# A fused attention and expert kernel: logits with the tokens in the rows, and the first expert's tokens selected in two parts

## The chip, the cores and the metric

The kernel runs on one core of one Trainium2 chip. The metric is the time in microseconds (us) that the device needs for one execution; less is better. The engines are TensorE (PE in the profile; its weight loads are listed apart as PEld), VectorE (DVE), ScalarE (ACT), GpSimd (POOL), and SyncE (SP), which issues most transfers. Each engine works off its own instructions in order and waits for the others on semaphores, so an instruction that has to wait holds everything that stands behind it on its engine.

## The reference, cut to what matters

Three stages follow each other: attention with a sliding window (2 x 8 heads, 768 positions, 64 wide), a dense layer pair on the resulting 1536 x 512 tokens, and a layer in which each token goes to one of eight experts, or to none.

```python
x = attention(q, k, v)               # 1536 tokens x 512
x = np.maximum(0.01 * (x @ w_in), x @ w_in) @ w_out        # 512 -> 2048 -> 512
do_compute = (x @ w_skip) > 0
logits = x[do_compute] @ w_gate      # 8 experts
e_idx = np.argmax(logits, axis=1)
gate_w = softmax(logits)[e_idx]
for e in range(8):                   # w1[e]: 512 x 1024, w2[e]: 1024 x 512
    h = np.maximum(xc[e_idx == e] @ w1[e], 0.0)
    y[e_idx == e] = gate_w * (h @ w2[e])
out = x;  out[do_compute] = x[do_compute] + y
```

All is float32. The kernel gets that precision from a faster product format (written fp32r in the rows) by cutting each operand into a high part and a low part, what the high part leaves over, and adding three products: high by high, low by high, high by low.

## The kernel before, in words

The 1536 tokens are six groups of 256, each two tiles of 128. While group g goes through the dense layers, the attention of group g+1 is done between its products. A group takes 16 chunks (`chunk`): 12 products of 256 columns into `h` (L835), four passes on ACT and DVE that make the high and low part of the activation, and six products of 512 columns into the two sums `acc`, one for each tile (L856). For the last four chunks of the last group the products into the second tile's sum are put off (`self.rest`), so that the first tile's sum is complete earlier.

When a group's sums are complete, `gating` works out where each token goes. The sums are copied to `x2`, one half by ACT (L902) and one by DVE (L904), and stored. PE transposes the tile (L918, four transposes), ACT and DVE make the high and low part `xh` of the transposed tile (L921, L922). Twelve products (L930) then take `w9`, the nine columns of `w_skip` and `w_gate`, as the weights and 128 tokens as the moving columns, so that the logits come out as 9 rows of 128 tokens; ACT copies them (L935), and PE transposes them back (L937), so that DVE finds the tokens in the rows. DVE takes the maximum (L947), the comparison with zero (L948), the first expert that has the maximum (L950, L952), and its one-hot row (L954). PE counts how many tokens of each expert stand ahead of each token (L977: products of bf16 ones and a triangle with the one-hot rows), DVE reads the token's rank out of the counts (L983), and POOL scatters the tokens to the experts' lists `scr` in DRAM (L994). The last group's two tiles go through `gating` one after the other.

An expert then reads its list `xs` back from DRAM. For the first expert that way round would be too long: its list as it stood before the last group is read ahead (`first_rows`), and the tokens of the last two tiles are added by products (`first_x`). `sel` holds for each tile a 128 x 128 matrix of zeros and ones, made by DVE from the ranks (L987), that puts the tile's tokens into the expert's slots. PE writes `xs` transposed into four sums, one for each quarter of the model width (L817: plain float32, four products, which run as two instructions each), and adds both tiles' tokens (L819: eight products, 16 instructions). ACT and DVE cut the four sums into high and low part `xt` (L1088, L1089), and the first expert's 24 products of 512 columns start (L1060).

The experts' weights come as 16 sets (two for each expert) of four chunks of 512 KB. SP loads each chunk into one of four buffers `wm`; ACT makes the high part (L701) and DVE, or POOL for the last chunk of a set, the low part (L708), into two of 32 buffers `w`. A chunk's `wm` buffer is free when its low part is made, and a `w` buffer when PE has used it. An expert's second layer is L1076.

The order on each engine isn't written out: every operation is entered with an engine, an assumed cost and a priority `pr` (`Plan.op`), a planner plays them through (`Plan.run`), starting on each engine the ready operation of least priority whose buffers are free, and the program is written in that order. So a change of one cost, dependence or buffer can move instructions on every engine from that place on.

## Time and profile before

| what | us |
|---|---|
| median of 3 runs | 563.36 (563.24 to 564.45) |
| the profiled execution | 565.15 |
| its span, from the first to the last instruction | 563.3 |
| PE busy | 523.5 (93%) |
| PE weight loads | 458.1 (81%) |
| DVE busy | 406.2 (72%) |
| ACT busy | 345.9 (61%) |
| POOL busy | 170.0 (30%) |
| chain that ended last: PE | 60% of the span |
| chain that ended last: DVE, ACT, DMA, POOL | 12%, 9%, 8%, 6% |

The profiled execution is one of its own and 1.79 us above the median of the three timed runs; durations are read from it, and differences are taken from the median. The span is almost the whole of its time. Busy times of PE overlap, since its products are pipelined: two products of 0.39 us that follow each other start 0.23 us apart. So the distance between starts is what counts.

### The profile page before, as it was taken

How to read it: one execution, taken by the hardware profiler on the slowest of the kernel's cores; microseconds unless marked ns; L12 is line 12 of the kernel's file. 1: busy time of each engine (PE TensorE's matmuls, PEld its weight loads, DVE VectorE, ACT ScalarE, POOL GpSimd, SP SyncE). 2: the span in 40 equal slices, each digit the busy share in tenths (PEclk: the TensorE clock that was granted, in tenths of full speed). 3: DMA queues.
4: the chain of work that ended last, by engine and by line, in shares of the span. 5: the costliest groups of instructions: out<-in, count | busy, mean ns of one | idle time of the engine just before them, and what ended most of it. 6: DMA issues, size and time to landing. Idle time of an engine off the chain costs nothing.

```text
span 563.3 us, 10312 instructions
## 1 busy us (share of the span) xinstructions
PE 523.5 (93%) x3370; PEld 458.1 (81%) x3370; DVE 406.2 (72%) x1160; ACT 345.9 (61%) x889; POOL 170.0 (30%) x285
## 2 busy tenths in 40 slices
PE   4899999999999999989999999999999889999993
PEld 2778998888888898978888888998887768888771
DVE  3899999997767677777577776756855566776761
ACT  3998766654665566675566765556456267666660
POOL 4322022130353143333233332220321214434343
PEclk9999999999999999999999999999999699999997
DMA  7998345330111112221112320117465277787870
GB/s 181 286 324 282 119 153 158 115 104 20 34 38 43 51 40 47 49 76 43 29 41 47 85 48 3 25 37 219 144 212 171 84 283 249 256 272 270 259 229 20
DMA packets 78912, 72.47 MB, mean 129 GB/s; under 512 B 56403, under 2 KB 64595, under 8 KB 78848
## 3 DMA queue, kind: packets, MB, share of 16 engines
q1 hardware_dynamic: 76560, 70.54, 40.8%
q0 software_dynamic: 1600, 1.04, 0.6%
q8 instruction: 29, 0.48, 0.3%
q14 instruction: 35, 0.29, 0.2%
q10 hardware_dynamic: 688, 0.13, 0.1%
HBM read 65.40 MB, written 10.51 MB: 135 GB/s over the span
## 4 chain that ended last, share of the span: by engine, by line
PE 60%; DVE 12%; ACT 9%; DMA 8%; POOL 6%; issue 4%; POOLq 0%; SPq 0%; ACTq 0%; DVEq 0%
PE h L835 17%; PE acc L856 14%; DMA wm<-in_moe_w_dram 5%; PE acc L1076 3%; PE PV L655 3%; PE T L616 3%; POOL w L708 3%; ACT P L588 2%; PE h L1060 2%; PE S L582 2%; PE S L1060 2%; PE T L930 2%; DVE C L671 1%; PE PV L1060 1%; DVE P L585 1%
## 5 line engine op out<-in xcount | busy, mean ns | idle before, releaser
L835 PE MATMUL h<-x,w 128*128 128x256 f32 x1128 | 155.2, 286 | 1.0 <-DVE gl L849 0.9
L835 PEld LDWEIGHTS h<-x,w 128*128 128x128 f32 x1128 | 144.0, 190 | 5.3 <-DVE gl L849 1.3
L856 PE MATMUL acc<-w,gh 128*128 128x512 f32 x308 | 100.1, 406 | 0.2 <-ACT gh L848 0.2
L701 ACT ACTIVATE w<-wm 128x1024 fp32r<-128x1024 f32 x64 | 67.9, 1061 | 43.9 <-DMA wm<-in_moe_w_dram 27.5
L708 DVE TENSOR_TENSOR w<-wm,w 128x1024 fp32r<-128x1024 f32 x48 | 61.9, 1302 | 20.6 <-ACT w L701 18.8
L588 ACT ACTIVATE P<-P,s 128x272 f32<-128x272 f32 (+1 forms) x96 | 50.1, 523 | 27.9 <-DVE s L585 26.8
L708 POOL TENSOR_TENSOR w<-wm,w 128x1024 fp32r<-128x1024 f32 x16 | 38.7, 2416 | 89.1 <-ACT w L701 47.6
L600 POOL TENSOR_SCALAR P<-P,s 128x272 f32<-128x272 f32 (+1 forms) x72 | 36.5, 518 | 93.8 <-DVE s L593 74.9
L856 PE MATMUL acc<-w,gl 128*128 128x512 f32 x156 | 61.4, 394 | 0.0
L856 PEld LDWEIGHTS acc<-w,gh 128*128 128x128 f32 x308 | 53.3, 189 | 8.0 <-ACT gh L848 0.6
L846 ACT ACTIVATE t<-h 128x256 f32<-128x256 f32 x94 | 35.6, 379 | 34.8 <-PE h L835 34.5
L847 DVE TENSOR_TENSOR h<-h,t 128x256 f32<-128x256 f32 x94 | 40.1, 427 | 20.8 <-ACT t L846 20.0
L848 ACT ACTIVATE gh<-h 128x256 fp32r<-128x256 f32 x92 | 34.8, 378 | 21.0 <-DVE h L847 20.4
L849 DVE TENSOR_TENSOR gl<-h,gh 128x256 fp32r<-128x256 f32 x92 | 38.5, 419 | 10.2 <-ACT gh L848 9.5
L585 DVE CUSTOM_DVE_ANT_0 P<-S,mk 128x272 f32<-128x272 f32 (+1 forms) x70 | 28.9, 413 | 11.4 <-PE S L582 7.9
L856 PEld LDWEIGHTS acc<-w,gl 128*128 128x128 f32 x156 | 29.3, 188 | 7.4 <-DVE gl L849 0.8
L616 PE MATMUL T<-idt,P 128*128 128x128 f32 x152 | 27.1, 295 | 7.1 <-DVE kT L503 3.2
L616 PEld LDWEIGHTS T<-idt,P 128*128 128x128 f32 x152 | 22.3, 205 | 13.0 <-POOL P L600 4.1
L672 POOL TENSOR_TENSOR xr<-C 128x128 f32<-128x128 f32 x32 | 15.6, 488 | 43.2 <-DVE C L671 43.0
L671 DVE TENSOR_TENSOR C<-PV,C 64x256 f32<-64x256 f32 x48 | 20.2, 422 | 11.2 <-ACT C L670 8.1
L622 ACT ACTIVATE AT<-T 128x256 fp32r<-128x256 f32 x60 | 20.0, 382 | 13.4 <-PE T L616 13.1
L623 DVE TENSOR_TENSOR AT<-T,AT 128x256 fp32r<-128x256 f32 x60 | 23.3, 419 | 6.0 <-ACT AT L622 5.7
(264 smaller groups left out, 1081.0 us busy)
## 6 DMA issues: line engine op xcount, KB each, us to landing
wm<-in_moe_w_dram SPq DMA_DIRECT2D x64, 512.0 KB, 4.7
w<-in_moe_w_in_dram SPq DMA_DIRECT2D x14, 512.0 KB, 6.3
w<-in_moe_w_out_dram SPq DMA_DIRECT2D x14, 512.0 KB, 7.3
rq<-in_q_dram SPq DMA_DIRECT2D x56, 64.0 KB, 2.2
out_dram<-x SPq DMA_DIRECT2D x12, 256.0 KB, 2.8
rk<-in_k_dram SPq DMA_DIRECT2D x24, 96.0 KB, 2.4
rv<-in_v_dram SPq DMA_DIRECT2D x24, 96.0 KB, 2.3
scr<-x SPq DMA_DIRECT2D x1, 2056.0 KB, 9.4
```

The costliest lines, as they stand in the source:

```text
L585: P.op("DVE", 66 + 1.07 * ncol, lambda sp=sp, h=h: nc.vector.tensor_tensor_reduce(out=A.tile[:, 0:ncol, h], in0=sp.tile[:, 0:ncol], in1=ma ...
L588: P.op("ACT", 280 + 0.83 * ncol, lambda h=h: nc.scalar.activation(out=A.tile[:, 0:ncol, h], in_=A.tile[:, 0:ncol, h], func=AF.Exp, scale=- ...
L600: P.op("POOL", 245 + 0.83 * ncol, lambda h=h: nc.gpsimd.tensor_scalar(out=A.tile[:, 0:ncol, h], in0=A.tile[:, 0:ncol, h], scalar1=sm.tile[ ...
L616: nc.tensor.transpose(tt.tile[:, 2 * j + h, :], A.tile[:, o:o + 128, h], c["idt"])
L701: nc.scalar.activation(out=at(0), in_=view(src.tile), func=AF.Copy)
L708: P.op(lo, {"DVE": c_dve(n), "POOL": c_pool2(n)}[lo], lambda: eng[lo].tensor_tensor(out=at(1), in0=view(src.tile), in1=at(0).bitcast(F32), ...
L835: nc.tensor.matmul(out=h.tile, lhsT=wi.tile[:, a, 128 * k:128 * k + 128], rhs=xT.tile[:, b, k, :], start=k == 0 and n == 0, stop=k == self ...
L846: P.op("ACT", c_act(256, True), lambda: nc.scalar.activation(out=t.tile, in_=h.tile, func=AF.Copy, scale=0.01), r=[h], w=[t], pr=fast)
L847: P.op("DVE", c_dve(256), lambda: nc.vector.tensor_tensor(out=h.tile, in0=h.tile, in1=t.tile, op=ALU.max), r=[t], w=[h], pr=fast)
L848: P.op("ACT", c_act(256, True), lambda: nc.scalar.activation(out=gh.tile, in_=h.tile, func=AF.Copy), r=[h], w=[gh], pr=fast)
L849: P.op("DVE", c_dve(256), lambda: nc.vector.tensor_tensor(out=gl.tile, in0=h.tile, in1=gh.tile.bitcast(F32), op=ALU.subtract), r=[h, gh], ...
L856: nc.tensor.matmul(out=acc[i].tile, lhsT=a.tile[:, q], rhs=wo.tile[:, b, :], start=first and n == 0, stop=last and n == 2)
```

## The change

The logits change sides: the tile `xh` becomes the weights and `w9`, widened by a column of zeros to ten, the moving columns. The result stands with the tokens in the rows at once, in one tile `lt`; the copy L935 and the transposes L937 go. Products that need only the high part of `xh` come first.

For the first expert, `xs` and the two tiles of tokens are cut into high and low part as rows, ahead of the selection (`split_rows`: ACT makes the high part, DVE the low part of `xs`, POOL that of the tiles), and the selection is done on both parts with fp32r products: 8 for each of the three sources, for two sums `hi` of two quarters each and one `lo`. What was the cut after the selection is now two copies by ACT and two by DVE. `sel` is made from the counts (`cp`) directly, ahead of the rank.

`idle` adds products of bf16 ones, 128 x 128, that nobody reads: 6 after the last product of the second tile's sum, 12 after its logits, 5 after its count, 5 after the selection. And the third and fourth chunk of the third expert's first set are cut only after the first expert's `xt` (`after=[first]`), the fourth one's low part by DVE, not POOL.

```diff
     def gating(self, g, acc, own):
...
-        lp = P.buf("T", [9, 128 * n])
+        lt = P.buf("T", [128, n, 10])
...
-            for h in range(parts):
-                ks = range(4 // parts * h, 4 // parts * (h + 1))
-
-                def lg(m=m, xh=xh, ks=ks):
-                    for k in ks:
-                        for j, (a, b) in enumerate(((0, 0), (1, 0), (0, 1))):
-                            nc.tensor.matmul(out=lp.tile[:, 128 * m:128 * m + 128], lhsT=self.w9[:, a, k, :], rhs=xh.tile[:, b, 128 * k:128 * k + 128],
-                                             start=k == 0 and j == 0, stop=k == 3 and j == 2)
-
-                P.op("PE", 3 * len(ks) * 54, lg, r=[(xh, (0, h)), (xh, (1, h)), "w9"], w=[lp], pr=pr)
-        ls = P.buf("wl", [9, 128 * n])
-        P.op("ACT", c_act(128 * n, True), lambda: nc.scalar.activation(out=ls.tile, in_=lp.tile, func=AF.Copy), r=[lp], w=[ls], pr=pr)
-        lt = P.buf("T", [128, n, 9])
-        P.op("PE", 30 * n, lambda: [nc.tensor.transpose(lt.tile[:, m, :], ls.tile[:, 128 * m:128 * m + 128], c["idt"][0:9, 0:9]) for m in range(n)], r=[ls], w=[lt], pr=pr)
+            for b, ws in ((0, (0, 1)), (1, (0,))):
+                for h in range(parts):
+                    ks = range(4 // parts * h, 4 // parts * (h + 1))
+
+                    def lg(m=m, xh=xh, ks=ks, b=b, ws=ws):
+                        for k in ks:
+                            for a in ws:
+                                nc.tensor.matmul(out=lt.tile[:, m, :], lhsT=xh.tile[:, b, 128 * k:128 * k + 128], rhs=self.w9[:, a, k, :],
+                                                 start=k == 0 and a == 0 and b == 0, stop=k == 3 and b == 1)
+
+                    made = P.op("PE", len(ws) * len(ks) * 57, lg, r=[(xh, (b, h)), "w9"], w=[lt], pr=pr)
+        if self.fast and last and own == [1]:
+            self.idle(12, made)
...
     def first_rows(self):
...
+        self.xa = P.buf("gT", [128, 2, 2, 4, 128], F32R)
+        self.split_rows(self.xs0, [self.xs0], self.xa, 0, lambda i: self.xa.tile[:, 0, i], pr)
+
+    def split_rows(self, x, rd, dst, n, at, pr, lo="DVE", after=()):
+
+        P, nc = self.p, self.nc
+        cols = lambda: x.tile[:, 0:512].rearrange("p (f k) -> p k f", k=4)
+        P.op("ACT", c_act(512, False), lambda: nc.scalar.activation(out=at(0), in_=cols(), func=AF.Copy), r=rd, w=[(dst, (n, 0))], pr=pr, after=after)
+        P.op(lo, c_dve(512) if lo == "DVE" else c_pool2(512), lambda: (nc.vector if lo == "DVE" else nc.gpsimd).tensor_tensor(out=at(1), in0=cols(), in1=at(0).bitcast(F32), op=ALU.subtract), r=rd + [(dst, (n, 0))], w=[(dst, (n, 1))], pr=pr)
+
+    def first_x(self, x2, high):
...
+        hi, lo = [P.buf("h", [128, 2, 128]) for _ in range(2)], P.buf("acc", [128, 2, 2, 128])
...
+                    P.op("PE", 2 * 60, lambda i=i, j=j: [nc.tensor.matmul(
+                        out=self.x0[i][j][2]()[:, k, :], lhsT=at(i)[:, 2 * j + k, :], rhs=sel.tile[:, col, :], start=n == 0 and k == 0 and not (i and j), stop=n == 2 and k == 1 and (j == 1 or not i)) for k in range(2)],
+                        r=[(x, (1 if n else 0, i))] + rd, w=[self.x0[i][j][0:2]], pr=pr)
...
+    def idle(self, n, done):
+
+        nc, x, ones = self.nc, self.spare, self.c["ones"]
+        self.p.op("PE", n * 57, lambda: [nc.tensor.matmul(out=x.tile[:, 0:128], lhsT=ones, rhs=ones, start=True, stop=True) for _ in range(n)], w=[x], pr=self.KF * self.NG, after=[done])
...
     def plan_routed(self):
...
-                self.split(raw, hl, lambda i, hl=hl: hl[i].tile, 1024, pr + 0.3 * n, "ACT", "DVE" if n != 3 else "POOL")
+                self.split(raw, hl, lambda i, hl=hl: hl[i].tile, 1024, pr + 0.3 * n, "ACT", "DVE" if n != 3 or (e, m) == (2, 0) else "POOL", after=[first] if (e, m) == (2, 0) and n > 1 else ())
...
-                for k, x in enumerate(self.x0):
-                    self.split_psum(x, (xt, k), lambda i, xt=xt, k=k: xt.tile[:, i, k], 128, N - 9)
+                for j in range(2):
+                    P.op("ACT", c_act(256, True), lambda xt=xt, j=j: nc.scalar.activation(out=xt.tile[:, 0, 2 * j:2 * j + 2, :], in_=self.x0[0][j][2](), func=AF.Copy), r=[self.x0[0][j][0:2]], w=[(xt, (2 * j, 0)), (xt, (2 * j + 1, 0))], pr=N - 9)
+                    first = P.op("DVE", c_dve(256), lambda xt=xt, j=j: nc.vector.tensor_copy(xt.tile[:, 1, 2 * j:2 * j + 2, :], self.x0[1][j][2]()), r=[self.x0[1][j][0:2]], w=[(xt, (2 * j, 1)), (xt, (2 * j + 1, 1))], pr=N - 9)
```

What the planner makes of it is shown at three places. On PE, around the last product of the second tile's sum: `acc_5663` is that sum before and `acc_5641` after, `T_6242` and `T_6214` hold the first tile's transposes, and L930 and L971 are the logits. Before:

```order
L856 MATMUL acc_5663<-w_1818,xr_6197 128x512 x2
L856 MATMUL acc_5663<-w_1818,gl_6209 128x512
L817 MATMUL acc_6238<-idt,xs_5967 128x128
L918 MATMUL T_6242<-idt,x_1270_5901 128x128 x4
L856 MATMUL acc_5663<-w_1892,gh_6204 128x512 x2
L856 MATMUL acc_5663<-w_1892,gl_6213 128x512
L930 MATMUL T_6258<-wl_6243,w_75 9x128 x6
L817 MATMUL acc_6266<-idt,xs_5967 128x128
L930 MATMUL T_6258<-wl_6243,w_75 9x128 x6
L918 MATMUL T_6277<-idt,x_1283_5965 128x128 x4
L937 MATMUL T_6284<-idt,wl_6275 128x9
L930 MATMUL T_6296<-wl_6278,w_75 9x128 x12
```

After (L893 is L856, L957 is L918, L840 the selection, L857 the products that nobody reads):

```order
L893 MATMUL acc_5641<-w_1809,xr_6179 128x512 x2
L893 MATMUL acc_5641<-w_1809,gl_6191 128x512
L957 MATMUL T_6214<-idt,x_1260_5880 128x128 x2
L893 MATMUL acc_5641<-w_1895,gh_6186 128x512 x2
L893 MATMUL acc_5641<-w_1895,gl_6198 128x512
L957 MATMUL T_6214<-idt,x_1260_5880 128x128 x2
L971 MATMUL T_6227<-w_75,wl_6215 128x10 x4
L840 MATMUL acc_6232<-hs_5483,gT_5969 128x128 x4
L971 MATMUL T_6227<-w_75,wl_6215 128x10 x6
L857 LDWEIGHTS ones
L857 MATMUL acc_6248<-ones 128x128
```

The product on `xs` and two of the four transposes no longer stand ahead of the sum's last three products, and the transposes back (L937) are gone.

On PE, between the count over all tiles (L1007, after: L1048) and the first expert's first product (L1060), which follows the eight L819 before, and after the four rows L840 and the products that nobody reads. `hs` is `sel`, and `x_1270`, `x_1283` and `x_6294` the last two tiles. Before:

```order
L1007 LDWEIGHTS ones
L1007 MATMUL T_6354<-oh_all,ones 128x8
L819 MATMUL h_6175<-hs_5603,x_1270_5901 128x128
L819 MATMUL h_6175<-hs_5603,x_1283_5965 128x128
L819 MATMUL h_6220<-hs_5603,x_1270_5901 128x128
L819 MATMUL h_6220<-hs_5603,x_1283_5965 128x128
L819 MATMUL acc_6238<-hs_5603,x_1270_5901 128x128
L819 MATMUL acc_6238<-hs_5603,x_1283_5965 128x128
L819 MATMUL acc_6266<-hs_5603,x_1270_5901 128x128
L819 MATMUL acc_6266<-hs_5603,x_1283_5965 128x128
L1060 MATMUL S_6397<-w_5659,wl_6383 128x512
```

After:

```order
L1048 LDWEIGHTS ones
L1048 MATMUL T_6358<-oh_all,ones 128x8
L840 MATMUL h_6156<-hs_5483,x_6294 128x128 x2
L840 MATMUL acc_6232<-hs_5483,x_6294 128x128 x2
L840 MATMUL h_6200<-hs_5483,x_6294 128x128 x2
L840 MATMUL acc_6232<-hs_5483,x_6294 128x128 x2
L857 LDWEIGHTS ones
L857 MATMUL acc_6248<-ones 128x128
```

Eight float32 products that read both tiles have become eight fp32r products that read the last tile's two parts; the other tile's stand further ahead.

On ACT, between the last exponential and the first expert's hidden rows. `wl_6383` is `xt`; `wm_6169`, `wm_6211`, `wm_6233` and `wm_6289` are the four chunks of the second expert's second set before. Before:

```order
L1088 ACTIVATE wl_6383<-h_6175 128x128
L1088 ACTIVATE wl_6383<-h_6220 128x128
L1088 ACTIVATE wl_6383<-acc_6238 128x128
L1088 ACTIVATE wl_6383<-acc_6266 128x128
L701 ACTIVATE w_6417<-wm_6169 128x1024
L701 ACTIVATE w_6427<-wm_6211 128x1024
L701 ACTIVATE w_6439<-wm_6233 128x1024
L701 ACTIVATE w_6449<-wm_6289 128x1024
```

After, `wm_6064` and `wm_6115` are the third and fourth chunk of the third expert's first set, and `wm_6150` and `wm_6193` the first two of the second expert's second set (its last two are not yet loaded):

```order
L1091 ACTIVATE wl_6383<-h_6156 128x256
L1091 ACTIVATE wl_6383<-h_6200 128x256
L701 ACTIVATE w_6406<-wm_6064 128x1024
L701 ACTIVATE w_6420<-wm_6115 128x1024
L701 ACTIVATE w_6427<-wm_6150 128x1024
L701 ACTIVATE w_6439<-wm_6193 128x1024
```

Four cuts became two copies, and two chunks of an earlier set have come in behind them: the splitting, and with it the loading, stands two chunks further back at this place.

## Rows read from the trace of the kernel before

**Rows 1.** The page's 40 slices of the span: granted clock in tenths, one digit each.
```profile
PEclk9999999999999999999999999999999699999997
```

**Rows 2.** Busy time by stretch: stretch, length, engines (instructions), PEclk, DMA share, GB/s.
```profile
120.00:430.00 310.00, 298.87 (x2096) 268.08 (x2095) 217.86 (x713) 188.06 (x544) 93.16 (x189) 1.00 0.24 67
430.00:440.00 10.00, 8.15 (x47) 6.25 (x45) 4.70 (x14) 4.47 (x9) 2.37 (x1) 0.98 0.54 168
440.00:450.00 10.00, 8.53 (x60) 7.95 (x61) 5.72 (x42) 1.98 (x9) 1.97 (x2) 0.51 0.19 68
453.00:463.00 10.00, 8.23 (x41) 6.27 (x40) 6.94 (x11) 6.54 (x9) 2.36 (x1) 1.00 0.92 332
463.00:503.00 40.00, 40.00 (x196) 33.61 (x195) 28.18 (x35) 26.95 (x34) 17.44 (x8) 1.00 0.82 268
```

**Rows 3.** Chain of waits in order of time: start us, length us, what.
```profile
452.32 0.68 PE PV L1060 x3
...
500.74 2.40 POOL w L708
...
517.22 2.42 POOL w L708
```

**Rows 4.** Timeline of the last token tiles: start, us, engine, line, operation [idle before].
```profile
433.42 0.38 ACT L902 ACTIVATE x<-acc 128x256 f32<-128x256 f32 x1 [1.37 <-PE acc L856]
...
433.83 0.43 DVE L904 COPY x<-acc 128x256 f32<-128x256 f32 x1 [0.53 <-ACT x L902]
...
434.31 0.73 PE L817 MATMUL acc<-idt,xs 128*128 128x128 f32 x2 [0.24 <-DVE x L904]
...
435.78 0.40 PE L856 MATMUL acc<-w,gl 128*128 128x512 f32 x1
...
438.04 0.60 PE L918 MATMUL T<-idt,x 128*128 128x128 f32 x4
...
440.20 1.44 PE L930 MATMUL T<-wl,w 128*9 128x128 f32 x12 [1.40 <-DVE sm L959]
...
441.74 0.27 ACT L935 ACTIVATE wl<-T 9x128 f32<-9x128 f32 x1 [1.35 <-PE S L977]
...
442.06 0.27 PE L937 MATMUL T<-idt,wl 9*128 9x9 f32 x1
...
442.57 0.16 DVE L947 TENSOR_REDUCE sm<-T 128x1 f32<-128x8 f32 x1
...
443.85 2.24 PE L819 MATMUL h<-hs,x 128*128 128x128 f32 x8
443.92 0.35 DVE L987 TENSOR_SCALAR hs<-hs,rank_all 128x128 f32<-128x128 f32 x1
...
447.62 1.63 PE L1060 MATMUL S<-w,wl 128*128 128x512 f32 x3
...
453.52 0.84 PE L1060 MATMUL PV<-w,wl 128*128 128x512 f32 x3
```

**Rows 5.** Timeline, PE at the full clock: small matmuls and transposes elsewhere.
```profile
181.51 0.34 PE L582 MATMUL S<-kT,qT 128*128 128x128 f32 x2
181.68 0.62 PE L918 MATMUL T<-idt,x 128*128 128x128 f32 x4
...
391.19 1.60 PE L930 MATMUL T<-wl,w 128*9 128x128 f32 x24
...
394.20 0.28 PE L937 MATMUL T<-idt,wl 9*128 9x9 f32 x2
...
428.01 0.50 PE L817 MATMUL h<-idt,xs 128*128 128x128 f32 x2
```

**Rows 6.** Timeline, where the stream of expert weights starts again.
```profile
450.07 1.06 ACT L701 ACTIVATE w<-wm 128x1024 fp32r<-128x1024 f32 x1 [1.79 <-PE PV L1060]
...
452.41 0.34 SPq L1031 DMA_DIRECT2D wm<-in_moe_w_dram  x1
```

**Rows 7.** The page's costliest groups: POOL's share of the weight splitting.
```profile
L708 POOL TENSOR_TENSOR w<-wm,w 128x1024 fp32r<-128x1024 f32 x16 | 38.7, 2416 | 89.1 <-ACT w L701 47.6
```

75 lines of the change are left out of this document (46 added, 29 removed).

## The prediction, as it was put on record before the changed kernel ran

> **What bounds the kernel now.** I read the slices first. Their clock digit is 9 nearly everywhere, with one 6 in slice 32 [rows 1]; that is the place to look at. The windows tell why. From 120 to 430 us PE is busy for 298.87 of 310 us at clock 1.00, so the body is bound by PE and holds 11.1 us in which PE does nothing. From 440 to 450 us the granted clock is 0.51, which is the lower level of 1.2 GHz, after a stretch with PE busy 8.15 of 10 us, and the DMA share is 0.19. From 463 to 503 us PE is busy for 40.00 of 40 us [rows 2]. The chain then shows what else is tight in that tail: beside PE it goes through the low parts that POOL makes of the expert weights, one every eight chunks, at 500.74 and 517.22, so a chunk takes (517.22 − 500.74)/8 = 2.06 us [rows 3]. PE and the weight stream run side by side there, both nearly full. Last I read the handover between body and tail in the timeline [rows 4]. It is a chain without slack: second tile's sum, logits, choice of expert, count, `sel`, selection, cuts, first expert.
>
> Four distances in it carry the sum [rows 4]. From the end of the second tile's sum (435.78 + 0.40 = 436.18) to the end of the transposed logits (442.06 + 0.27 = 442.33): 6.15 us. From the maximum (442.57) to the end of `sel` (443.92 + 0.35 = 444.27): 1.70. From there to the first product of the first expert (447.62): 3.35, most of it the eight plain float32 products, which take 2.24. The expert's 24 products, to 453.52 + 0.84 = 454.36: 6.74.
>
> **The change part by part.**
>
> *The body.* The transposes back of five earlier pairs of tiles go, 0.28 us each pair at most; they overlap with their neighbours, so I count 0.2, together −1.0 (bounds 0 and −1.4). Their copy on ACT lies beside PE work. Two of the four products on `xs` stood in the body at 0.50 each (two instructions) [rows 5]; for all four now come eight fp32r ones, at some 0.06 by the same rows: 8 × 0.06 − 2 × 0.50 = −0.5. The logits remain 12 a tile, but with 128 columns as weights and 10 moving. Before, 24 of them took 1.60, a pitch of about (1.60 − 0.22)/23 = 0.060, where 0.22 is what a single one takes from its start to its end. The trace has no product with 128 columns of weights and ten moving. The nearest is the fp32r product of 128 by 128 in the attention: two of them start at 181.51 and the next instruction starts at 181.68, so a weight load and a product of 128 columns take 0.085 at most [rows 5]. I take 0.060, no change; at 0.085, 120 of them in the body would cost 120 × 0.025 = 3.0, and half of the 11.1 us in which PE is idle might swallow some.
>
> The Trainium skill, page "TensorE: Matmul & The Clock Gate", section "LDWEIGHTS (loading the stationary operand)", has the load's time grow with the columns loaded, 1.2 of them a ns: 128 columns would take an estimated 107 ns, however few columns move, and that speaks against just this part, which loaded nine before. By it the body's logits would cost an estimated 120 × 47 ns = 5.6 us more. The 85 ns for load and product of 128 by 128 disagree [rows 5].
>
> *The second tile's sum.* Ahead of its last products stood the first `xs` product (0.73 us) and four transposes, which now are two [rows 4]. At full clock four transposes take 0.44 or so, from the 0.62 for the group less the end of the last [rows 5], so two are 0.2. The sum is complete 0.73 + 0.2 = 0.9 earlier; with the wait of 0.24 in front of the product I take −1.0.
>
> *From the sum to the logits.* The copy (0.27) and the transpose back (0.27), with their handover from 441.74 to 442.33, go: −0.6. The 12 logit products took 1.44 at the half clock; at the full one half of that, −0.72 [rows 4]. For that the clock must stay up: six products that nobody reads follow the sum and 12 more stand behind the logits, each some 0.06 us by the nearest row above, in waits that are idle before (1.40 ahead of the logits). Against it I put 0.1 to 0.2, since low part and `sel` of the first tile now stand on DVE near the same time. −1.2 (bounds −0.6 and −1.5).
>
> *From the logits to `sel`.* The rank no longer stands ahead of `sel`, the comparison with zero moves behind the candidates; a DVE instruction of this size is 0.16 [rows 4]. −0.1.
>
> *From `sel` to the first expert.* The 2.24 of float32 products become eight fp32r ones for the last tile, 8 × 0.06 = 0.5; the first tile's and `xs`'s stand earlier, in PE's waits. ACT then copies 256 columns (0.38 for the same size by the copy of `x2`) and DVE 256 (0.43) [rows 4]. Together 0.95 against 3.35: −2.4 (bounds −1.6 and −2.7). New on this path is POOL, which makes the low part of the tile's rows, 512 columns. Its row for 1024 columns is 2.42 us, half of that 1.2 [rows 7]. It starts with the tile's high part on ACT, some 3 us ahead of the selection, and the two tiles' parts follow each other; I cost them at nothing. Were the cover gone, the selection would wait for up to one such part, 1.2.
>
> *The first expert's 24 products.* Three take 1.63 at the half clock and 0.68 at the full one [rows 3, 4]. So 8 × 0.68 = 5.44 against 6.74: −1.3.
>
> *The weight stream.* This term goes the other way. After the first expert's start, ACT cuts the next chunk as soon as PE frees a `w` buffer (450.07), and SP issues the next load when a `wm` buffer is free (452.41, 4.8 us after the expert's first product) [rows 4, 6]. Before, DMA does little from 440 to 450 (share 0.19, 68 GB/s), so the four `wm` and 32 `w` buffers are likely full when the expert starts. Now two chunks wait for `xt`: the stream stands two further back, 2 × 2.06 = 4.1 us of work. It gets part back. Those two chunks need no buffer from PE, so ACT cuts them right behind `xt`, about 0.5 after the expert's start; from the cut at 450.07 to the next load it took 2.34 [rows 6], so the loads start some 2.9 after the expert's start, not 4.8: 1.9 sooner. And from 453 to 463 us the transfers ran at 332 GB/s against 268 behind, so the stream can run quicker than PE uses it for a while [rows 2]. The bounds are 0, if PE stays the bound throughout, and 3.5, if the tail is the stream's alone: all that stands ahead of this term is −7.5, of which −1.3 lies behind the expert's start, so the stream starts 6.2 + 1.9 = 8.1 sooner with 4.1 more to do, and gains 4.0. By the row with PE at 40.00 of 40 [rows 2] PE is nearer, so I take +0.9.
>
> *The order of the body* changes on every engine from the planner. I give it no term and ±1.5, from the 11.1 us of PE's idle time.
>
> *Sum.* −1.0 − 0.5 − 1.0 − 1.2 − 0.1 − 2.4 − 1.3 + 0.9 = −6.6. The profiled execution takes 565.15, a span of 563.3 and 1.8 around it; it becomes 558.55. It stands 1.79 above the median of 563.36, so the median becomes 563.36 − 6.6 = 556.8.
>
> **The rivals.**
>
> *The clock falls nevertheless.* It fell after a stretch with PE 82% busy [rows 2], and the new waits are filled by 0.06 us a product, 28 of them: 1.7 us into some 5 us of waits. Then 0.72 (logits), 0.4 (selection) and 1.3 (first expert) are lost again: 559.2. For it: six and 12 short products don't fill a wait of 1.4 and those behind it. Against it: the float32 products go, and the path itself has shorter waits.
>
> *The stream decides the tail.* Then the gain is the 4.0 worked out above: 559.4. For it: the chain's POOL steps [rows 3]. Against it: PE at 40.00 of 40.
>
> *The logits cost their weight loads* (slower). If a load of 128 columns can't be hidden behind ten moving columns, the pitch rises. 120 products in the body and 24 late ones, at a pitch p, cost 144 × (p − 0.060): against −6.6 that breaks even at 0.106, and is slower than before by more than 0.2% from 0.114. The transposes, which also load 128 columns, stand in the body at 0.62 for four, less the 0.22 of the last 0.13 each [rows 5]: at 0.13 the cost is 10.1, and the time 566.9. For it: that row, though plain float32 is slower in these rows anyway (two instructions of L817 take 0.50, two fp32r products 0.34). Against it: 0.085 for 128 by 128.
>
> *The logits cost about what the rest gains.* The same mechanism with a pitch from 0.098 to 0.114: at 0.106, midway between the 0.085 of the fp32r pair and the 0.13 of the transposes, the time is 563.4.
>
> The rule of the Trainium skill named above is this case: its 107 ns would give an estimated 563.6.
>
> *The body's new order eats the gain.* 430 us of work are planned anew, with 11.1 us of idle time to win or lose: 563. Against it: most of the gain stands behind the body, on a path without slack.
>
> **How the numbers follow.** My forecast has 0.54 (its own range 554.5 to 558.9), the clock 0.20, the stream 0.10, the slower logits 0.08, logits that cost what the rest gains 0.03, the body's order 0.02, and 0.03 a time under 554.5, if the stream gives nothing back and the body's order turns out well. Less than 0.2%, 1.1 us, can't be told from no change. Faster are the first three and the last, together 0.87; the same are the two before the last, 0.05; slower 0.08. The range goes from 554.3 to 561.0: it holds the forecast, and the clock's and the stream's case with their uncertainty of 1.5 upward.
>
> **What would show it.** The clock digit in slice 32 stays at 9, and the window of ten us behind the second tile's sum has 1.00 for 0.51: the clock's part. 12 logits at ten columns take about 0.7, and 24 in the body 1.6: the pitch. The first expert's first product comes about 6.2 earlier than 447.62 (4.7 of the handover, 1.5 of the body), and its 24 products take 5.4. The start of the last chunks' low parts comes by less than that, if the stream holds. The prediction is wrong if the logits stand at over 0.1 each in the body, if the selection waits for POOL's low part, or if from the first expert on PE has waits on ACT's or POOL's cut that it didn't have.

## The result, and the profile after

The change made the kernel slower: 569.62 us against 564.47, medians of 20 runs each, ratio 1.0083 (95% interval 1.0062 to 1.0104). Forecast were 556.8 and a range to 561.0. (The forecast started from 563.36, the median of three runs; from 564.47 its −6.6 would lead to 557.9.) The profiled executions understate the difference (567.08 against 565.15): that of the changed kernel lies 2.5 under its median, that of before 0.7 above its own, so the profile serves to place the loss, and the runs to size it.

The clock by slices [rows 1 for before] and by stretches [rows 2]:

```profile
PEclk9999999999999999999999999999999799999997
```

```profile
120.00:430.00 310.00, 301.14 (x2069) 271.69 (x2068) 216.36 (x710) 185.49 (x536) 94.84 (x191) 1.00 0.24 66
430.00:440.00 10.00, 9.77 (x69) 7.97 (x68) 4.68 (x12) 4.40 (x11) 0.61 (x1) 1.00 0.45 158
440.00:450.00 10.00, 9.53 (x84) 8.90 (x83) 7.97 (x45) 4.82 (x11) 4.42 (x4) 0.66 0.06 22
```

PE was forecast to be freed in the body, and it is busier: 301.14 us of 310, so 8.86 idle where 11.13 were. From 440 to 450 the clock is 0.66 and not the forecast 1.00: it fell again, only later. The half clock lasts from 443.3 to 450.1 us, where before it lasted from 439.6 to 449.8. And the DMA engines, at 0.19 there before, are at 0.06.

The logits, ten columns moved against 128 of weights, at the full clock in the body; the number at the start of a row, its start, is what counts, since products overlap. After:

```profile
144.38 2.74 PE L971 MATMUL T<-w,wl 128*128 128x10 f32 x24
146.98 0.44 PE L526 MATMUL T<-idt,rq 128*128 128x128 f32 x2
```

and before, the same place:

```profile
143.55 1.60 PE L930 MATMUL T<-wl,w 128*9 128x128 f32 x24
144.99 0.38 PE L526 MATMUL T<-idt,rq 128*128 128x128 f32 x2
```

From the first of 24 to what follows them it is 2.60 us after and 1.44 before: 0.108 a product for 0.060 (within the row the products start 0.112 apart). Over the five pairs of tiles in the body it is 12.85 for 7.40.

The handover, with the rows that answer to [rows 4] (L893 is the second tile's sum, L943 its copy, L957 the transposes, L971 the logits, L840 the selection, L857 the fillers, which are the products that nobody reads, L986 the maximum, L1026 `sel`, L826 a tile's low part as rows on POOL, L1033 the slot indices, L1102 the first expert):

```profile
436.81 0.40 PE L893 MATMUL acc<-w,gl 128*128 128x512 f32 x1
...
437.66 0.42 DVE L943 COPY x<-acc 128x256 f32<-128x256 f32 x1 [0.28 <-ACT x L941]
...
438.08 0.64 PE L840 MATMUL acc<-hs,gT 128*128 128x128 f32 x4
...
438.56 0.78 PE L971 MATMUL T<-w,wl 128*128 128x10 f32 x6
...
439.20 0.51 PE L857 MATMUL acc<-ones 128*128 128x128 bf16 x6
...
439.52 0.36 PE L971 MATMUL T<-w,wl 128*128 128x10 f32 x2
...
439.74 0.66 PE L957 MATMUL T<-idt,x 128*128 128x128 f32 x4
...
442.38 1.52 POOL L826 TENSOR_TENSOR x<-x,x 128x512 fp32r<-128x512 f32 x1 [1.45 <-ACT x L825]
...
442.71 1.21 DVE L1033 SCALAR_TENSOR_TENSOR sm<-rank_all,sm 128x1 int32<-128x1 f32 x1
...
443.25 0.51 PE L971 MATMUL T<-w,wl 128*128 128x10 f32 x2
...
443.84 0.15 DVE L986 TENSOR_REDUCE sm<-T 128x1 f32<-128x8 f32 x1
...
445.17 0.35 DVE L1026 TENSOR_SCALAR hs<-wf,PV 128x128 fp32r<-128x128 f32 x1
...
445.81 0.67 PE L840 MATMUL h<-hs,x 128*128 128x128 f32 x2
...
447.13 0.63 PE L840 MATMUL acc<-hs,x 128*128 128x128 f32 x2
...
448.08 1.63 PE L1102 MATMUL S<-w,wl 128*128 128x512 f32 x3
...
453.91 0.84 PE L1102 MATMUL PV<-w,wl 128*128 128x512 f32 x3
```

Five distances can be laid beside those of before. To the end of the second tile's sum: 437.21, 1.0 later than before. From there to the end of the logits (443.76, read from the two at 443.25): 6.55 for 6.15. From the maximum to the end of `sel`: 1.68 for 1.70. From there to the first expert: 2.56 for 3.35. Its 24 products, to 454.75: 6.67 for 6.74. So the first expert starts at 448.08, 0.46 later than before, where 6.2 earlier was forecast; and from the end of its products to the end of the span, in what is called the tail here, it is 110.6 for 109.0.

Between the products, three things stand out. The second tile's rows are in `x2` at 438.08, but its transposes start at 439.74: the first tile's logits, four products of the selection and the six of L857 stand ahead of them on PE. And L1033, 0.22 in the other places, takes 1.21 while POOL makes a low part (442.38 to 443.90), and both end together. It cost the path next to nothing, since the logits that the maximum needs ended only at 443.76. And `sel` ends at 445.52, 1.6 behind POOL's low part, so the selection didn't wait for that one.

From 450 to 557 us, PE's waits for the low parts of the weights (L708) have grown. Before, and after:

```profile
PE acc L1076 <- POOL w L708: 1.6, 1, 1.6
...
PE acc L1076 <- DVE w L708: 0.5, 2, 0.3
```

```profile
PE acc L1118 <- POOL w L708: 2.3, 2, 1.6
...
PE h L1102 <- POOL w L708: 1.1, 1, 1.1
...
PE acc L1118 <- DVE w L708: 0.6, 1, 0.6
```

The numbers are the us in total, how often, and the longest: 4.0 for 2.1. The prediction named such waits as a sign that it is wrong.

### The profile page after: what moved, and what is told of

Its sections match the earlier page's. It is cut to its first block, busy times and chain, and to the rows that moved or that the text cites. A ratio compares the mean times of both kernels' runs of the same rounds, so it can differ in the third digit from the quotient of the medians.

```text
span 565.3 us, 10354 instructions
## 1 busy us (share of the span) xinstructions
PE 528.5 (93%) x3386; PEld 464.1 (82%) x3386; DVE 407.0 (72%) x1161; ACT 346.2 (61%) x884; POOL 168.2 (30%) x286
## 5 line engine op out<-in xcount | busy, mean ns | idle before, releaser
L893 PE MATMUL acc<-w,gh 128*128 128x512 f32 x308 | 99.7, 405 | 0.0
L708 DVE TENSOR_TENSOR w<-wm,w 128x1024 fp32r<-128x1024 f32 x49 | 62.4, 1284 | 18.3 <-ACT w L701 16.8
L893 PE MATMUL acc<-w,gl 128*128 128x512 f32 x156 | 61.4, 394 | 0.0
L893 PEld LDWEIGHTS acc<-w,gh 128*128 128x128 f32 x308 | 53.3, 189 | 7.4
L600 POOL TENSOR_SCALAR P<-P,s 128x272 f32<-128x272 f32 (+1 forms) x72 | 37.7, 535 | 71.8 <-DVE s L593 60.0
L708 POOL TENSOR_TENSOR w<-wm,w 128x1024 fp32r<-128x1024 f32 x15 | 36.0, 2399 | 59.5 <-ACT w L701 38.8
L893 PEld LDWEIGHTS acc<-w,gl 128*128 128x128 f32 x156 | 29.3, 188 | 7.6 <-DVE gl L886 1.0
L701 ACT ACTIVATE w<-wf 128x512 fp32r<-128x512 f32 x32 | 20.1, 629 | 13.2 <-DVE wf L741 11.6
```

The source lines that it names most:

```text
L600: P.op("POOL", 245 + 0.83 * ncol, lambda h=h: nc.gpsimd.tensor_scalar(out=A.tile[:, 0:ncol, h], in0=A.tile[:, 0:ncol, h], scalar1=sm.tile[ ...
L701: nc.scalar.activation(out=at(0), in_=view(src.tile), func=AF.Copy)
L708: P.op(lo, {"DVE": c_dve(n), "POOL": c_pool2(n)}[lo], lambda: eng[lo].tensor_tensor(out=at(1), in0=view(src.tile), in1=at(0).bitcast(F32), ...
L893: nc.tensor.matmul(out=acc[i].tile, lhsT=a.tile[:, q], rhs=wo.tile[:, b, :], start=first and n == 0, stop=last and n == 2)
```

## The experiments

Thirteen kernels ran. The theories, by number: 1, weight loads of 128 columns set the logits' pitch (the distance between the starts of two products) and the body pays; 2 and 8, the fillers hold the clock; 3, putting two chunks back costs the tail; 4, the memset of the tenth column moves the body's order; 5, the logits' new side pays for the last tiles; 6, the selection in two parts gains nothing on the path; 7, the weight stream sets the end, whenever the first expert starts.

| kernel | median, us | kernel before beside it | ratio (95% interval) | median granted clock |
|---|---|---|---|---|
| the changed kernel | 569.62 | 564.47 | 1.0083 (1.0062 to 1.0104) | 0.9845 |
| 1: its body with old logits | 568.02 | 564.84 | 1.0054 (1.0028 to 1.0080) | 0.9835 |
| 2: before + new logits | 566.35 | 564.84 | 1.0041 (1.0017 to 1.0066) | 0.9875 |
| 3: changed, no fillers | 567.88 | 564.84 | 1.0060 (1.0034 to 1.0087) | 0.985 |
| 4: changed, no chunks put back | 571.86 | 564.84 | 1.0124 (1.0091 to 1.0156) | 0.979 |
| 5: as 1, no memset | 565.74 | 563.81 | 1.0032 (1.0015 to 1.0049) | 0.984 |
| 6: before + new logits of the last two tiles | 563.62 | 563.81 | 0.9998 (0.9968 to 1.0028) | 0.989 |
| 7: changed, old logits | 566.91 | 563.81 | 1.0052 (1.0028 to 1.0075) | 0.986 |
| 8: as 2, no memset | 568.42 | 563.81 | 1.0084 (1.0048 to 1.0120) | 0.9815 |
| 9: as 7, no chunks put back | 563.93 | 565.12 | 0.9988 (0.9956 to 1.0019) | 0.994 |
| 10: as 7, no fillers | 564.34 | 565.12 | 0.9996 (0.9974 to 1.0019) | 0.9865 |
| 11: before + chunks put back | 566.77 | 565.12 | 1.0025 (1.0000 to 1.0050) | 0.9875 |
| 12: as 7, neither | 564.89 | 565.58 | 0.9998 (0.9973 to 1.0023) | 0.983 |
| 13: as 5, no chunks put back | 567.36 | 565.58 | 1.0034 (1.0009 to 1.0059) | 0.983 |

The ratios and their intervals are worked out from all runs of both kernels, so a ratio need not equal the quotient of the two medians (for kernel 2 that would be 1.0027). The last column is the mean granted clock of an execution, its median over the runs; for the kernel before it was 0.986 to 0.989 beside the experiments. A clock lower by 0.003 over these 565 us is 1.7 us of PE's time by estimate, so part of a difference between medians can be the clock's.

Read from the profiles, in us from the span's start. Some executions begin their first layer product 1.7 to 1.9 later than the 24.8 of before; that delay of each is taken off, so that the columns can be compared. Each row is one execution.

| kernel | start of the last first-layer product of the body | end of the second tile's sum | start of the first expert | end of the last product on PE |
|---|---|---|---|---|
| before | 426.5 | 436.2 | 447.6 | 555.5 |
| changed | 428.9 | 437.1 | 448.0 | 557.2 |
| 1 | 427.5 | 435.8 | 447.7 | 558.4 |
| 2 | 429.0 | 438.7 | 448.9 | 554.4 |
| 3 | 429.0 | 437.2 | 448.0 | 558.3 |
| 4 | 429.2 | 437.4 | 449.1 | 558.4 |
| 5 | 426.1 | 434.4 | 446.5 | 557.5 |
| 6 | 426.7 | 436.4 | 447.4 | 555.0 |
| 7 | 426.3 | 434.6 | 444.7 | 557.3 |
| 8 | 430.1 | 439.8 | 450.7 | 555.9 |
| 9 | 426.9 | 435.2 | 445.6 | 554.2 |
| 10 | 426.4 | 434.7 | 445.4 | 554.6 |
| 11 | 426.7 | 436.4 | 447.9 | 559.0 |
| 12 | 426.2 | 434.4 | 445.6 | 554.3 |
| 13 | 426.7 | 435.0 | 446.9 | 557.7 |

**1. The body's logits back on the old side.**

```diff
+            if not rows:    # rows: the last two tiles
+                P.op("PE", 12 * 54, lg9, ...)    # w9 the weights, 128 columns moving
+                continue
```

> The changed kernel, but the five pairs of tiles in the body take their logits the old way (nine columns as the weights, 128 moving, copy and transposes back); the last two tiles keep the new way. Theory 1 (a weight load of 128 columns sets the pitch: 0.112 us a product against 0.060): 120 products in the body get 0.052 each back, 6.2, less the five pairs of transposes back, 1.0: the sum of the last group comes about 5 us earlier than in the changed kernel, and the time is about 5 lower, level with the kernel before or a little better (ratio 0.995 to 1.001). Rival A (the planner's new order of the body is what costs, the pitch is hidden in PE's idle time): the body stays within 1.5 of the changed kernel, ratio 1.005 to 1.009. Rival B (the clock in the handover and the tail is what makes the timed runs slow): body as theory 1 in part, ratio over 1.004.

The body came 1.4 earlier, not 5: the logits' side is not the whole of its delay, and theory 1's size was wrong as a price in time. The time went down by 1.6, and the two intervals overlap.

**2. The new logits alone**, in the kernel before (the memset with them).

```diff
-                nc.tensor.matmul(out=lp..., lhsT=self.w9[:, a, k, :], rhs=xh.tile[:, b, ...])
+                nc.tensor.matmul(out=lt.tile[:, m, :], lhsT=xh.tile[:, b, ...], rhs=self.w9[:, a, k, :])
```

> The kernel before with nothing but the logits changed to the new side, for all tiles; selection, fillers and weight stream as before. Theory 1: 120 x 0.052 = 6.2 more in the body less 1.0 for the transposes back; in the handover the last tile loses the copy and the transpose back (0.6) and pays 12 x 0.05 = 0.6: about 5 us slower, ratio 1.007 to 1.010. Rival A (order): within 2 us of the kernel before, ratio 0.997 to 1.003.

Slower, but by half of what theory 1 said; the body is 2.5 late, as in the changed kernel. The last product on PE nevertheless ends 1.1 earlier than before, which no theory had foretold. In this profile the half clock lasts from 443.5 to 450.4, 6.8 us where it is 10.2 before; that is worth up to an estimated 1.7 of PE's time. And the profiled execution, with 564.06, lies 2.3 under the kernel's median.

**3. No fillers.**

```diff
-            self.idle(6, done)
-            self.idle(12, made)
-                self.idle(5, P.ops[-1])
-            self.idle(5, self.p.ops[-1])
```

> The changed kernel without the 28 products that nobody reads. If they hold the clock up (theory 2: it fell at 443.3 instead of 439.8 thanks to them), the clock falls some 3 us earlier in the handover and the first expert starts 1 to 1.5 later: 0.5 to 1.5 slower than the changed kernel, ratio to the kernel before 1.009 to 1.012. Rival C (they do nothing for the clock, and the six ahead of the second tile's transposes only stand in the way): the first expert starts 0.3 to 0.5 earlier, ratio 1.005 to 1.008.

The clock fell earlier (at 442.6 for 443.3; 0.63 from 440 to 450 for 0.66), the first expert started when it had, and the time is not higher: 567.88 against 569.62, the intervals overlap. Theory 2's price is refuted in this kernel.

**4. No chunks put back.**

```diff
-"DVE" if n != 3 or (e, m) == (2, 0) else "POOL", after=[first] if (e, m) == (2, 0) and n > 1 else ())
+"DVE" if n != 3 else "POOL")
```

> The changed kernel, with the third expert's third and fourth chunk cut as before the change, ahead of the handover and not behind it. Theory 3 (the stream of weights, put back by two chunks, costs the 1.5 us that are lost between the end of the first expert's first layer and the start of the second expert): the second expert's first product comes about 1.5 earlier and the time is 1.5 lower, ratio 1.004 to 1.007. Rival D (PE sets the end, or the cuts then stand in the handover's way on ACT and DVE): the same as the changed kernel within 0.5, ratio 1.007 to 1.010, or slower.

Theory 3 fell in this form: not faster, and by the medians of five runs and twenty slower still, though the intervals overlap. The first expert started 1.1 later than in the changed kernel, and in its profile the products of 512 columns run at the half clock twice, in the first expert's first layer and again from 462 to 465 us. PE's waits for the weights did shrink, to 1.9.

**5. The memset gone**, with the body's old logits.

```diff
-        P.op("DVE", 70, lambda: nc.vector.memset(raw.tile, 0.0), w=[raw], pr=8, after=[done])
+            nc.sync.dma_start(out=raw.tile[:, :, 9:10], in_=io["moe2_w_skip"]...)    # third small transfer
```

> The changed kernel with the old logits in the body, and without the memset that makes the tenth column: a third small transfer fills it with w_skip again (a column that nobody reads). The body's instructions then stand in the order of the kernel before up to the last group. Theory 4 (the memset on DVE moved the order of the early body and cost 1.1 to 1.2, and the pitch of the logits the other 1.2 of the 2.4 that the changed kernel's body is late): the body's last first-layer product starts within 0.4 of the kernel before (426.5 from the span's start, unless the start of the run shifts), 1.2 ahead of the run with the memset; time 1 to 1.5 under that run, ratio 1.002 to 1.005. Rival A (the order after the memset is not the cause): body still 1.1 late, ratio 1.005 to 1.007.

Theory 4 held: one small DVE instruction near 95 us, with the dependence of the transfers on it, had moved the planner's order, and without it the body ends 1.4 sooner and level with before. The body's loss is all between this kernel and the changed one: 2.8, and as much in the ratios (1.0083 and 1.0032). These two differ in the body's logits and in the memset.

**6. The new logits for the last two tiles alone**, in the kernel before. Edit: `rows = last` in `gating` chooses the side.

> The kernel before with the new logits for the last two tiles alone (no memset, the tenth column as a third small transfer); selection, weight stream and body as before. Theory 5 (the new side pays where the path waits for it: no copy and no transpose back, while its pitch costs 12 x 0.052 = 0.6): from the second tile's sum to the first expert 10.3 for 11.4, time 1 to 2 under the kernel before, ratio 0.996 to 0.999. Rival E (the pitch takes back what the copy gave, or the tail eats it): ratio 0.999 to 1.002.

The first expert starts 0.2 earlier, not 1.1, and the time is the same. The copy and the transpose back were worth what the slower logits cost.

**7. Selection, fillers and put-back chunks with the old logits.** Edit: the logits of `gating` as before the change.

> The changed kernel with the old logits for all tiles: selection in two parts, fillers and the third expert's put-back chunks alone. Theory 6 (the selection in two parts gains nothing on the path, since the rows' high and low parts, the fillers and the first tile's products stand ahead of the second tile's transposes, and the tail loses 1.3 to 1.5 behind the first expert): sum to first expert 11 to 12, ratio 1.003 to 1.007. Rival F (the forecast's mechanism: the selection gains 2.4, and only the logits spoil it): sum to first expert under 9.5, ratio 0.994 to 0.999.

This run decides most. Theory 6 and rival F were both wrong in part: the handover did gain, sum to first expert 10.1 for 11.4, and the first expert starts 2.9 earlier than before; yet the last product comes 1.8 later. The clock did not fall in the handover:

```profile
430.00:440.00 10.00, 7.98 (x63) 6.37 (x63) 4.88 (x15) 4.96 (x12) 2.55 (x2) 1.00 0.30 109
440.00:450.00 10.00, 8.94 (x84) 7.70 (x84) 8.27 (x40) 5.09 (x8) 2.46 (x3) 1.00 0.13 41
450.00:463.00 13.00, 10.17 (x48) 7.58 (x47) 7.67 (x12) 6.41 (x8) 2.39 (x1) 1.00 0.93 327
```

From 440 to 450 it is 1.00, with PE at 8.94, and the DMA share is 0.13. The handover could have gained more. The first tile's one-hot rows (L994) take 1.53 for the 0.23 of the second tile's, end together with a low part on POOL, and PE waits 1.00 for them; the other rows are the end of `sel` and the first expert's products:

```profile
438.96 1.52 POOL L826 TENSOR_TENSOR x<-x,x 128x512 fp32r<-128x512 f32 x1 [0.64 <-ACT x L825]
438.98 1.53 DVE L994 SCALAR_TENSOR_TENSOR oh_all<-em,sm 128x8 bf16<-128x8 f32 x1
...
440.56 0.17 PE L1017 MATMUL S<-oh_all,tri 128*128 128x8 bf16 x1 [1.00 <-DVE oh_all L994]
...
443.07 0.35 DVE L1027 TENSOR_SCALAR hs<-wf,PV 128x128 fp32r<-128x128 f32 x1
...
444.69 0.71 PE L1103 MATMUL S<-w,wl 128*128 128x512 f32 x2
...
445.90 0.50 PE L1103 MATMUL S<-w,wl 128*128 128x512 f32 x1 [0.50 <-DVE wl L1093]
...
450.31 0.84 PE L1103 MATMUL PV<-w,wl 128*128 128x512 f32 x3
```

What follows is loads and cuts:

```profile
444.68 2.00 ACT L701 ACTIVATE w<-wm 128x1024 fp32r<-128x1024 f32 x2
...
448.08 1.48 SPq L1073 DMA_DIRECT2D wm<-in_moe_w_dram  x2
...
449.60 0.90 SPq L1086 DMA_DIRECT2D xs<-scr  x2
...
450.60 0.38 SPq L1073 DMA_DIRECT2D wm<-in_moe_w_dram  x1
451.03 0.53 SPq L1086 DMA_DIRECT2D xs<-scr  x1
...
452.09 1.06 ACT L701 ACTIVATE w<-wm 128x1024 fp32r<-128x1024 f32 x1 [0.98 <-DMA wm<-in_moe_w_dram]
...
455.66 1.06 ACT L701 ACTIVATE w<-wm 128x1024 fp32r<-128x1024 f32 x1 [1.54 <-DMA wm<-in_moe_w_dram]
...
459.01 1.06 ACT L701 ACTIVATE w<-wm 128x1024 fp32r<-128x1024 f32 x1 [0.54 <-DMA wm<-in_moe_w_dram]
```

ACT cuts the two put-back chunks at 444.68, and the loads begin at 448.08. Then ACT waits three times for a load (`<-DMA wm`): the cut at 459.01, the 21st, comes when it did before (458.98), though the expert started 2.9 sooner. The 64th and last cut comes at 552.21, 2.4 later than before (549.84). Not all of that is the stream's: PE waits 2.2 us for ACT, up to 530.4, and then runs at the half clock from 531.3 to 534.7, which is worth up to an estimated 1.7. The 38th slice shows it with an 8:

```profile
PEclk9999999999999999999999999999999999999897
```

The 49th cut, ahead of that wait, was 1.7 late already (521.1 for 519.4).

**8. The new logits without the memset**, in the kernel before. Edit: as in 5, a third small transfer fills the tenth column.

> The kernel before with the new logits for all tiles, without the memset. Theory 4: of 120 x 0.052 = 6.2 less 1.0 some 5.2 are added to PE's work in the body, of which PE's idle time there takes about 4, as with the changed kernel (PE idle from 120 to 430 us: 8.9 for 11.1): the body's last first-layer product is 1.0 to 1.5 late, and with the last tiles' gain of 1.2 the time is level with the kernel before, ratio 0.999 to 1.003. Rival A2 (nothing is hidden): body 4 to 5 late, ratio 1.005 to 1.008. Rival A3 (all is hidden): body level, ratio 0.996 to 0.999.

The body is 3.6 late, nearer to nothing hidden than forecast, and by the medians slower than with the memset, though the intervals overlap. The delay is not the products' price alone. In this profile two slices of the body have the clock digit 8: PE runs at the half clock from 148.2 to 151.6 and from 189.2 to 192.6, which together is worth up to an estimated 3.4 of PE's time.

```profile
PEclk9999999999899899999999999999999799999997
```

The runs show the same: 564.41 and 564.58 at clocks of 0.984 and 0.990, 571.71 to 572.72 at 0.976 and 0.977.

**9. As 7, no chunks put back.**

> Selection in two parts and fillers with the old logits, and the third expert's third and fourth chunk cut ahead of the handover as in the kernel before. Theory 7 (the stream of weights sets the end, whenever the first expert starts; put back by two chunks it ends 2 to 3 later): the end comes 2 to 3 earlier than with the chunks put back (565.2 span in its profile), ratio 0.998 to 1.002. Rival G (the two cuts on ACT and DVE or POOL stand in the handover's way, or the clock falls for it): first expert 1 to 3 later than 444.7, and the time as with the chunks put back or worse, ratio 1.004 or more.

As theory 7 said: the first expert 0.9 later than in 7, the last product 3.1 earlier, the time lower by 0.6% of before. The clock stays at 1.00 through the handover here too:

```profile
430.00:440.00 10.00, 9.64 (x71) 7.38 (x69) 5.79 (x12) 6.51 (x14) 2.88 (x2) 1.00 0.65 207
440.00:450.00 10.00, 7.57 (x86) 6.63 (x87) 7.39 (x44) 3.82 (x11) 4.49 (x4) 1.00 0.24 76
```

The profiled execution has a mean clock of 0.994. Of the twelve runs seven have 0.994 to 0.996 and a median of 562.46, 2.7 under the median of the kernel before beside it; the other five have 0.977 to 0.987 and 566.65. Where the clock fell in those five no profile shows.

**10. As 7, no fillers.**

> Selection in two parts with the old logits and the put-back chunks, without the 28 products that nobody reads. Theory 8 (the fillers do hold the clock where the handover is short enough): without them the clock falls between 436 and 446 and the first expert starts 1.5 to 3 later than the 444.7 with them. Theory 7 (the stream sets the end): the time stays within 1 of the 566.9 with fillers all the same, ratio 1.003 to 1.007. Rival H (PE sets the end): the time rises by the 1.5 to 3 as well, ratio 1.007 to 1.010.

Theory 8 held for the clock, and the rest failed. Without the fillers the clock is 0.66 from 440 to 450 where it was 1.00, the pairs of the selection's last products start 0.43 to 0.49 apart for 0.22 to 0.27, and the first expert starts 0.7 later, not 1.5 to 3. But the time is 0.6% lower, not level and not higher: PE's last product comes 2.7 earlier. Two things differ in the tail. This profile has no stretch at the half clock near 531, and the order on SP is another, which the planner had changed with the fillers' costs:

```profile
448.63 2.60 SPq L1066 DMA_DIRECT2D wm<-in_moe_w_dram  x3
...
451.29 0.90 SPq L1079 DMA_DIRECT2D xs<-scr  x2
...
455.90 1.06 ACT L701 ACTIVATE w<-wm 128x1024 fp32r<-128x1024 f32 x1 [0.86 <-DMA wm<-in_moe_w_dram]
...
457.25 1.06 ACT L701 ACTIVATE w<-wm 128x1024 fp32r<-128x1024 f32 x1 [0.29 <-DMA wm<-in_moe_w_dram]
```

Three loads of weights now stand ahead of the first two lists `xs`, where with the fillers it was two, and the 21st cut comes at 457.25 for 459.01. Which of the two brings the 2.7 wasn't tried apart.

**11. The chunks put back, alone**, in the kernel before.

```diff
+                    first = P.ops[-1]    # the last cut of the first expert's tokens
-"DVE" if n != 3 else "POOL")
+"DVE" if n != 3 or (e, m) == (2, 0) else "POOL", after=[first] if (e, m) == (2, 0) and n > 1 else ())
```

> The kernel before with one change: the third expert's third and fourth chunk are cut only behind the first expert's last cut. Theory 7: the first expert starts when it did (447.6 within 0.5), the cuts from the 23rd on come 2 to 4 later, and so does the end by 2 to 3.5: ratio 1.003 to 1.006. Rival I (the tail is PE's): the cuts come later, but PE waits for none of them, and the time is the same within 0.7.

In the profile as theory 7 says: first expert within 0.3 of before, the 23rd cut 3.5 later, the last product 3.4 later. The runs show less, 1.0025, with an interval down to no change; the profiled execution, with 570.34, is the slowest of the twelve.

**12. Selection alone**: neither fillers nor put-back chunks.

> Selection in two parts alone: old logits, no fillers, no chunks put back. Theory 7 with the fillers' price taken off: the stream runs as in the kernel before, the first expert starts 1 to 2.5 earlier than in it, and of that 0 to 1.5 reaches the end: ratio 0.996 to 0.999. Rival G (without the fillers the clock falls in the handover, and the two cuts stand in its way): first expert no earlier than in the kernel before, ratio 0.999 to 1.003.

First expert 2.0 earlier, last product 1.2 earlier, time the same as before: what reaches the end is below what the runs can tell. Theory 7's ratio, 0.999 at most, isn't shown.

**13. The changed kernel without its two dearest parts**: old logits in the body, no chunks put back.

> Selection in two parts, fillers, and the new logits for the last two tiles alone (no memset); old logits in the body, no chunks put back. It is the changed kernel less the two parts that cost most by theories 1 and 7. Theory 7: 5.1 of the changed kernel's loss are its body (2.8) and its stream (2 to 3), so this one is level with the kernel before or up to 1.5 better: ratio 0.996 to 1.001. Rival G2 (the logits' weight loads in the handover and the cuts on ACT and DVE make it longer, and the clock falls): ratio 1.003 or more.

The rival came true, if only just by its ratio. With the new logits of the last tiles the clock falls near 440 in spite of the fillers, and once more in the first expert's second layer (457.6 to 461.0).

None of these versions beats the kernel before by more than its interval.

## Why the prediction was wrong, step by step

The failed step comes first, with its words: "I take 0.060, no change", for the logits' pitch. The price of one product was 0.108. Five pairs of tiles at 12.85 for 7.40 are 5.4 more; the transposes back take off 1.0, counted as forecast, and PE's idle time took 2.3 (11.13 to 8.86): 2.1, against 2.4 measured in the body. The order that the memset sets moves the body as well, 1.4 with the old logits (runs 1 and 5), so that this sum is not the only one that fits: taking the new logits out of the body gives 1.4 back with the memset in place (run 1), and 2.8 together with it (run 5). Run 8, without the memset, can't be laid beside run 2 for this, since its body ran at the half clock twice.

The bound of 0.085 was misread from [rows 5]: it went from product to product and left out that the first load runs under the product ahead. The weight loads of that place, in the kernel before, show it:

```profile
181.39 0.31 PEld L582 LDWEIGHTS S<-kT,qT 128*128 128x128 f32 x2
181.64 0.42 PEld L918 LDWEIGHTS T<-idt,x 128*128 128x128 f32 x4
```

Two loads of 128 columns lie between 181.39 and 181.64: some 0.125 each. Read that way, the row would have spoken for the two rivals with a slower pitch, at 0.08 and 0.03, and not against them. The measured pitch lies within the rival at 0.03, which kept the time level because it granted the rest of the forecast its 6.6; most of that did not come either. The Trainium skill's rule in "TensorE: Matmul & The Clock Gate", section "LDWEIGHTS (loading the stationary operand)", that a load takes the columns divided by 1.2 in ns, an estimated 107 ns, agrees with the measured 0.108; it was weighed against a row that had been misread.

*Sum earlier by 1.0, `xs` by 0.5.* Right: from the last first-layer product to the end of the sum it is 8.3 for 9.7, so −1.4. The eight products on `xs` cost some 0.11 each and not 0.06, but four of them now stand behind the sum.

*Sum to logits, −1.2.* Wrong: +0.4. The copy and the transpose went, but the logits' 12 products at the new pitch took their place (in run 6, with nothing else changed, the first expert gains 0.2), and the second tile's transposes started 1.7 after the tile was in `x2`, behind work of the first tile and fillers.

*Logits to `sel`, −0.1.* Right within the reading (−0.02).

*`sel` to first expert, −2.4.* A third of it, −0.8, because the clock was down. The eight products, taken at 0.06 each, have weights of 128 columns too: from 445.81 to the end of the last pair 1.95 at the half clock, and in run 7 at the full one some 1.1. In run 7 the whole distance is 1.27 (443.42 to 444.69), so −2.1: with the clock up, this term was nearly right.

*The clock, −1.3.* The condition of the rival at 0.20 came true: 24 products in 6.67, not 5.44. Even where the clock held, 5.44 was out of reach: in run 7 they take 6.46 (444.69 to 451.15), since the first ones now wait for DVE's copy (0.50 at 445.90). The fillers hold the clock in the profiles of runs 7 and 9, and not with the new logits in the last tiles (changed kernel, runs 1, 4, 5 and 13: 0.53 to 0.74 from 440 to 450). Without fillers it fell in all eight kernels, before included. Why the new logits bring it down isn't shown.

*The stream, +0.9.* The second failed step: "By the row with PE at 40.00 of 40 PE is nearer". PE is busy there, and yet the chunks put back make it wait behind. From 450 to 557 us PE waits 2.8 to 4.8 us for the cuts of weights in the seven kernels with put-back chunks, and 1.6 to 2.4 in the eight without. In the changed kernel it is 4.0 for 2.1, and its tail is 1.6 longer. How much of such waits reaches the time is not settled. Of the five pairs that differ in the put-back chunks alone, 7 and 9 differ by 0.6% and 11 and before by 0.25%; 10 and 12 are level, and so are 5 and 13; and the changed kernel is, by the medians, faster than 4. The clock blurs it: the profiles of 4 and 13 have a second stretch at the half clock soon behind the first expert's first layer, and those of 5 and 7 one late in the tail (548.3 to 551.7 and 531.3 to 534.7). Starting the first expert 2.0 to 2.9 us earlier, as 7, 9, 10 and 12 do, brought no gain clear of the interval. Starting it later is another matter: in their profiles 2 and 8, with the first expert 1.3 and 3.1 later, end PE's work within 1.1 of before, but their runs are slower by 0.4% and 0.8%. What sets the 2.1 us of a chunk in the tail (the transfers at a share near 0.82, the cuts, or the four `wm` buffers between them) stays open; more buffers weren't tried.

The sum of the profiled execution: body +2.43, to the second tile's sum −1.41, handover −0.56, expert −0.07, tail +1.63: +2.02 of span. The runs' 5.1 are more by the different places of the two profiles among their runs, and by the clock. The two profiled executions have a clock of 0.989 after and 0.984 before; over the runs the medians stand the other way round, 0.9845 after and 0.9875 before (the 26 runs beside kernels 1 to 4). Among runs of like clock, 0.987 to 0.989, the changed kernel's seven have a median of 567.22 and the 46 of before, of all 108 beside the experiments, 564.72: 2.5 apart. So about half of the loss goes with the lower clock; in which stretches of those runs it falls isn't on record.

## What to carry to other kernels

Swapping the operands of a small product changes which side is loaded: count 0.108 us at the full clock for each load of 128 fp32r columns, and measure it from load to load, not from product to product. Before shortening a handover, look whether a transfer stream starts behind it and whether anything in the change holds that stream back; an engine that reads 100% busy in one stretch may wait for it in the next. Look at the granted clock of every run before a difference of medians is put down to an edit. And where a planner sets the order, a 0.09 us instruction or a filler far away can be worth more than a part of the change: undo those first.

## What the runs showed of the hardware that was not expected

Loads of 128 columns: fp32r products start 0.112 apart with 10 columns moving and about as far with 128 (the four of L840 from 438.08 to 438.56: 0.12), bf16 ones 0.053 (the six of L857 from 439.20 to 439.52). With nine columns of weights and 128 moving it is 0.060. So here the load sets the pitch.

A DVE instruction on 128 x 1 elements took 1.21 us for 0.22 while POOL worked on 128 x 512 (L1033 above, and 1.22 in run 13); in run 7, where POOL was done, it took 0.22. There the one-hot rows met POOL, 1.53 for 0.23, and so they did in runs 9, 10 and 12, each time with 1.0 of waiting on PE. Each of these ended within 0.03 of POOL's instruction, while L1031 ran in 0.14 beside it (442.53 in the changed kernel): some DVE instructions are held until POOL is done, and others not. Which, and why, wasn't tried by itself. The prediction had costed POOL's low parts at nothing.

The clock fell in the changed kernel at 443.3, with PE at 9.77 from 430 to 440, and stayed up in run 7 with PE at 7.98 there. More busy time ahead of a wait did not hold it.
